# A grouped-query attention block with cached keys and values: how the last unit is divided and turned, and how the result is copied and stored

## The chip, the cores and the metric

The kernel runs on one core of one Trainium2 chip. The metric is the device time of one execution in microseconds; lower is better. A profiled execution gives a span (first to last instruction) and its own time, which is a little longer.

## The reference

Eight sequences, four new tokens each (32 token rows), 32 query heads that share 8 key/value heads, 2048 cached keys, head width 128. Everything is bf16.

```python
B, Sq, D = 8, 4, 512
Hq, Hkv, Sk, Dh = 32, 8, 2048, 128
q = (x @ wq).reshape(B, Sq, Hq, Dh).transpose(0, 2, 1, 3)
k = jnp.repeat(k_cache, 4, axis=1)
v = jnp.repeat(v_cache, 4, axis=1)
scores = jnp.einsum("bhqd,bhkd->bhqk", q, k) * (Dh ** -0.5)
p = softmax(scores, axis=-1)
o = jnp.einsum("bhqk,bhkd->bhqd", p, v)
return o.transpose(0, 2, 1, 3).reshape(B, Sq, Hq * Dh) @ wo
```

## The kernel before

The work is cut into 16 units. A unit is one sequence and four key/value heads: 64 query rows (four heads, each with 16 rows) against 2048 keys per head. Its keys and its values are 2 MB each and come in one transfer each; with `wq` and `wo` (4 MB each) the kernel reads 75.5 MB.

Per unit, the stages are: VectorE turns the keys in two halves (line 134), TensorE makes the scores, for one half of the keys on PSUM rows 0 to 63 and for the other half on rows 64 to 127 (L203), VectorE takes the maxima (L221 to L227), ScalarE the exponentials with their sums (L239), VectorE turns the probabilities (L249), and ScalarE, GpSimd and for the last unit VectorE spread them into a block form (L259). GpSimd adds the sums (L213, L272), VectorE inverts them (L277). Then 32 products accumulate the values into one PSUM tile `o_ps` (L288), 128 rows by two blocks of 128 columns. Of this tile two quarters are wanted: rows 0 to 63 of block 0 and rows 64 to 127 of block 1.

`divide` (L298 to L306) takes just these two quarters: two instructions of 64x128, each multiplied by the inverse sum of its row, into `o_sc` of 128x128. It is ScalarE's for units 0 to 13 and VectorE's for units 14 and 15. `finish` (L308 to L315) multiplies `o_sc` in fp32 by `both`, a 128x64 matrix that is the sum of the two halves of an identity (`ident4[:, :64] + ident4[:, 64:]`, L128). So the product turns `o_sc` and adds its two row halves in one go. The trace shows each fp32 product as two weight loads and two matmuls. A copy (L312) moves the result to `oT`; for units 13, 14 and 15 it is ScalarE's.

The order of instructions on each engine is the order of the program text, which the author wrote out by hand (`manual_schedule`). The unit loop runs 18 turns; in turn n the scores are of unit n and the values of unit n − 2. In the last turn the order is: values of unit 15, `finish(14)`, `divide(15)`. After the loop come, in this order: four row steps of the output projection (`project(0, 0, 4)`), `finish(15)`, four more row steps, then `to_tokens(1)` (eight transposes of `oT` into `nat`, two copies on ScalarE and VectorE, L330), four row steps, `to_wo_rows(1)` (eight products into `perm`, two copies, L348), and all the remaining row steps. A row step is two products of 32 output rows by 256 columns (L356), one for each half of the output columns, so the result `out_ps` stands as 64 rows by 256 columns. The weights `wo` arrive in six pieces issued by SyncE (L101); the last three hold 5, 2 and 1 row steps, and the last row step needs the last piece.

At the end two copies move `out_ps` to `out_sb`, one for each half of the columns: ScalarE, then VectorE (L419). Two stores follow: ScalarE's queue writes rows 0 to 31 into the left half of the output (L420), SyncE's queue rows 32 to 63 into the right half (L421).

Of the kernel before, what the change touches and what calls it, by code (L numbers as in the profile page):

```python
# [9 lines left out]
FP32 = mybir.dt.float32  # L10
# [4 lines left out]
def kernel(  # L15
# [9 lines left out]
    nc = tc.nc  # L25

    B, Sq, D = x.shape
    _, Hkv, Sk, Dh = k_cache.shape
# [3 lines left out]
    T = B * Sq  # L32
# [5 lines left out]
    NQ = G * HQ  # L38
# [4 lines left out]
    DH = D // 2  # L43
    NU = (Hkv // G) * B
# [14 lines left out]
    small = ctx.enter_context(tc.tile_pool(name="small", bufs=2))  # L59
# [13 lines left out]
    ident4 = const.tile([128, 128], FP32, name="ident4")  # L73
    both = const.tile([128, NQ], FP32, name="both")
# [3 lines left out]
    out_sb = const.tile([2 * T, DH], BF16, name="out_sb")  # L78
# [53 lines left out]
    def turn_keys(u, t):  # L132
        kts[(u, t)] = ktpool.tile([128, CT, 2, S, 2], BF16, tag="kt", name="kt")
        nc.vector.transpose(  # L134
            kts[(u, t)][:, :, :, :, :].rearrange("k c h s e -> k (c h s e)").bitcast(FP32),
            ks[u][:, t * CT : (t + 1) * CT, :].rearrange("s c d -> s (c d)").bitcast(FP32),
        )
# [11 lines left out]
    def q_products(hq):  # L149
        psq = psum_m.tile([128, rep * Dh], FP32, tag="m", name="psq")  # L150
        for r in range(R):
            for g in range(G):
                c0 = (hq * G + g) * rep * Dh
                nc.tensor.matmul(  # L154
                    psq[g * T : (g + 1) * T, :],
                    lhsT=xT_sb[:, r, :],
                    rhs=wq_sb[:, r, c0 : c0 + rep * Dh],
                    start=(r == 0),
                    stop=(r == R - 1),
                )  # L160
        return psq
# [10 lines left out]
    def spread_q(hq, q_nat, engines):  # L172
        q_t = small.tile([128, rep, 4, B, Sq], BF16, tag="q_t", name="q_t")
        nc.vector.transpose(  # L174
            q_t[:, :, :, :, :].rearrange("w h i b s -> w (h i b s)"),
            q_nat[:, :, :, :].rearrange("t n e w -> t (n e w)"),
        )
        for g in range(G):
            rows = slice(g * S, (g + 1) * S)
            engines[g](  # L180
                out=q_bd[rows, hq, :, :, :, g, :].rearrange(
                    "w k e b (h s) -> w (k e b) h s", h=rep
                ),
                in_=q_t[rows, :, :, :, :].rearrange("w h i b s -> w (i b) h s"),
            )
# [10 lines left out]
    def scores(u, t):  # L196
        hq, b = units[u]
        if t == 0:
            s_pss[u] = psum_s.tile([128, NT, CT // 2, S], FP32, tag="s", name="s_ps")
        for i in range(4):  # L200
            k, e = i // 2, i % 2
            for h in range(2):
                nc.tensor.matmul(  # L203
                    s_pss[u][h * NQ : (h + 1) * NQ, t, :, :],
                    lhsT=q_bd[:, hq, k, e, b, :, :].rearrange("k g q -> k (g q)"),
                    rhs=kts[(u, t)][:, h * CT // 2 : (h + 1) * CT // 2, k, :, e],
                    start=(i == 0),
                    stop=(i == 3),
                )
# [7 lines left out]
    def maxima(u):  # L217
        top = small.tile([128, 1], FP32, tag="top", name="top")
        swapped = small.tile([128, 1], FP32, tag="swapped", name="swapped")
        less[u] = small.tile([128, 1], FP32, tag="less", name="less")  # L220
        nc.vector.reduce_max(  # L221
            out=top[:, :],
            in_=s_pss[u][:, :, :, :].rearrange("q t c s -> q (t c s)"),
            axis=AX,
        )
        swap_halves(nc.vector, swapped, top)
        nc.vector.tensor_scalar(  # L227
            out=less[u][:, :],
            in0=swapped[:, :],
            scalar1=top[:, 0:1],  # L230
            scalar2=-1.0,
            op0=mybir.AluOpType.max,
            op1=MULT,
        )
# [12 lines left out]
    def probs_to_keys(u):  # L247
        p_t = small.tile([128, C // 4, 2, HQ, 2], BF16, tag="p_t", name="p_t")
        nc.vector.transpose(  # L249
            p_t[:, :, :, :, :].rearrange("s x g q j -> s (x g q j)").bitcast(FP32),  # L250
            s_sbs[u][:, :, :, :].rearrange("q a s j -> q (a s j)").bitcast(FP32),
        )
        by = [nc.scalar.copy, nc.gpsimd.tensor_copy] * G
        if u == NU - 1:
            by = [nc.vector.tensor_copy, nc.gpsimd.tensor_copy, nc.scalar.copy] * 3
        for h in range(2):
            for g in range(G):
                quad = 2 * h + g // 2
                by[h * G + g](  # L259
                    out=probs[u % PB][g * S : (g + 1) * S, h, :, :, g, :],  # L260
                    in_=p_t[quad * S : (quad + 1) * S, :, g % 2, :, :].rearrange(
                        "s x q j -> s x j q"
                    ),
                )

    r_sbs = {}

    def sums(u):
        swapped = small.tile([128, 1], FP32, tag="l_swapped", name="l_swapped")
        total = small.tile([128, 1], FP32, tag="l_total", name="l_total")  # L270
        swap_halves(nc.gpsimd, swapped, l_sbs[u])
        nc.gpsimd.tensor_tensor(out=total[:, :], in0=l_sbs[u][:, :], in1=swapped[:, :], op=ADD)  # L272
        return total

    def inverses(u, total):
        r_sbs[u] = totals.tile([128, 1], FP32, tag="r_sb", name="r_sb")
        nc.vector.reciprocal(r_sbs[u][:, :], total[:, :])  # L277

    o_pss = {}
    o_scs = {}  # L280

    def values(u, quarter):
# [3 lines left out]
        for a in range(CT // 4):  # L286
# [8 lines left out]
                stop=(c == C - 2),  # L295
            )

    def divide(u):  # L298
        o_scs[u] = small.tile([128, Dh], FP32, tag="o_sc", name="o_sc")
        for h in range(2):  # L300
            rows = slice(h * NQ, (h + 1) * NQ)
            to, of, by = o_scs[u][rows, :], o_pss[u][rows, h, :], r_sbs[u][rows, 0:1]
            if u < NU - LAG:
                nc.scalar.mul(out=to, in_=of, mul=by)  # L304
            else:
                nc.vector.tensor_scalar_mul(out=to, in0=of, scalar1=by)  # L306

    def finish(u):  # L308
        hq, b = units[u]
        o_t = psum_m.tile([128, NQ], FP32, tag="m", name="o_t")  # L310
        nc.tensor.matmul(o_t[:, :], lhsT=o_scs[u][:, :], rhs=both[:, :], start=True, stop=True)  # L311
        (nc.vector.tensor_copy if u < NU - LAG - 1 else nc.scalar.copy)(  # L312
            out=oT[hq][:, :, :, b, :].rearrange("d h p s -> d p h s"),
            in_=o_t[:, :].rearrange("d (p h s) -> d p h s", p=2, h=HP),
        )  # L315
# [49 lines left out]
    for n in range(NU + LAG):  # L365
        w = n - LAG
        if 0 < n <= NU:
            total = sums(n - 1)
        if 0 < n < NU:
            turn_keys(n, 0)  # L370
            turn_keys(n, 1)
        if n < NU:
            scores(n, 0)
        if w >= 1 and n < NU:
            finish(w - 1)
        if n < NU:
            scores(n, 1)
        if n == 2:
            q_ps = q_products(1)
        if n == 3:  # L380
            spread_q(1, q_nat, [by_gpsimd] * G)
        if 0 < n <= NU:
            probs_to_keys(n - 1)
            inverses(n - 1, total)
        if n < NU:
            maxima(n)
            exponentials(n)
        if n == 2:
            q_nat = scale_q(q_ps)
        if w == B + 1:  # L390
            to_tokens(0)
        if w == B + 2:
            to_wo_rows(0)
        if w >= 0:
            for quarter in range(4):
                values(w, quarter)
            if n >= NU:
                finish(w - 1)
            divide(w)
        load_ready(min(n + 1, NU), max(w + 1, 0))  # L400
        if n == NU - 1:
            assert not loads, loads
            for piece in pieces:
                load_wo(*piece)

    out_ps = psum_s.tile([2 * T, DH], FP32, tag="s", name="out_ps")
    half = WR // 2
    project(0, 0, half)
    finish(NU - 1)
    project(0, half, half)  # L410
    to_tokens(1)
# [2 lines left out]
    project(1, half, half)  # L414
    for piece in pieces[2:]:
        project(*piece)
    o2 = out.flatten_outer_dims()
    for c0, copy in ((0, nc.scalar.copy), (DH // 2, nc.vector.tensor_copy)):
        copy(out=out_sb[:, c0 : c0 + DH // 2], in_=out_ps[:, c0 : c0 + DH // 2])  # L419
    nc.scalar.dma_start(out=o2[:, :DH], in_=out_sb[:T, :])  # L420
    nc.sync.dma_start(out=o2[:, DH:], in_=out_sb[T:, :])  # L421


# [28 lines left out]
```

## Time and profile before

| | us |
|---|---|
| runs shown | 185.2, 190.14, 190.29 (median 190.14) |
| profiled execution, its own time | 185.48 |
| its span | 183.7 |
| keys turned, VectorE L134 | 72.0 busy |
| values, TensorE L288 | 62.9 busy |
| division, ScalarE L304 (64x128) | 0.363 each, 28 of them |
| division, VectorE L306 (64x128) | 0.350 each, 4 of them |
| last values end, first `out_ps` product starts | 174.2, 174.3 |
| last product of L356 ends | 180.6 |
| stores issued | 181.2 |

How lines of the profile are read here: a line of the timeline has the start in us from the span's start, the busy time of the merged instructions, the engine (PE is TensorE, PEld its weight loads, DVE is VectorE, ACT ScalarE, SP SyncE; a q behind the name is its DMA issue), the source line, the operation, the tile written and the tiles read, the shape, and how many. In brackets stands how long the engine was idle before and what ended that. "Issue" means that the profile shows nothing that was waited for. A line of transfers has the size and the us from issue to landing.

### The profile page before, as it was taken

The page shows a single profiled execution, that of the slowest core. Times are in us where ns is not written, and L with a number is a line of the kernel's source. Part 1 is how long each engine was busy: PE and PEld are TensorE (multiplying, and loading weights), DVE is VectorE, ACT ScalarE, POOL GpSimd, SP SyncE. Part 2 cuts the span into 40 slices and gives each one's busy share as a digit, 9 for nine tenths or more (in the row PEclk, how much of TensorE's full clock was granted, in tenths as well). Part 3 has the DMA queues.
Part 4 walks back from the last instruction along what each step waited for, and adds up shares of the span by engine and source line. Part 5 has one row for each costly group of instructions (what it writes and reads, how often), then busy time and mean ns, then how long its engine had stood idle before and what let it go on. Part 6 is the DMA issues. An engine that isn't in the chain of part 4 may idle for free.

```text
span 183.7 us, 2500 instructions
## 1 busy us (share of the span) xinstructions
PE 122.7 (67%) x932; PEld 79.9 (44%) x932; DVE 119.8 (65%) x157; ACT 77.5 (42%) x136; POOL 59.4 (32%) x127
## 2 busy tenths in 40 slices
PE   0000470739996887839597839596776988399993
PEld 0000130213774664626354615455463656268871
DVE  4180209796999989494958677676958594946220
ACT  2000203435565754907263634547281619074020
POOL 8900011425175451605151513232231506056000
PEclk9999998556999999996969997969997599969999
DMA  6999999999999999999999999999999999999990
GB/s 189 460 421 407 435 432 432 428 432 432 428 435 421 441 417 437 426 432 432 425 435 428 432 428 435 425 432 432 432 432 428 432 425 439 425 432 416 426 366 26
DMA packets 5770, 75.70 MB, mean 412 GB/s; under 512 B 672, under 2 KB 896, under 8 KB 1152
## 3 DMA queue, kind: packets, MB, share of 16 engines
q1 hardware_dynamic: 5712, 75.55, 96.8%
q8 instruction: 7, 0.11, 0.2%
q10 hardware_dynamic: 48, 0.02, 0.0%
q14 instruction: 3, 0.02, 0.0%
HBM read 75.53 MB, written 0.03 MB: 411 GB/s over the span
## 4 chain that ended last, share of the span: by engine, by line
DMA 56%; DVE 26%; PE 12%; issue 3%; POOL 1%; ACT 0%; SPq 0%
DMA k_sb<-in_k_cache_dram 39%; DVE kt L134 19%; DMA x_sb<-in_x_dram 9%; DMA v_sb<-in_v_cache_dram 8%; PE s_ps L203 5%; DVE top L221 3%; PE o_ps L288 2%; PE out_ps L356 2%; PE psq L154 1%; DVE swapped L213 1%; POOL q_bd L180 1%; DVE q_t L174 1%; DVE less L227 1%; DVE o_sc L306 0%; PE perm L341 0%
## 5 line engine op out<-in xcount | busy, mean ns | idle before, releaser
L134 DVE STREAM_TRANSPOSE kt<-k_sb 128x2048 f32<-128x2048 f32 x32 | 72.0, 2288 | 21.7 <-DMA k_sb<-in_k_cache_dram 21.7
L203 PE MATMUL s_ps<-kt,q_bd 128*64 128x512 bf16 x256 | 45.0, 483 | 38.5 <-DVE kt L134 35.5
L288 PE MATMUL o_ps<-v_sb,probs 128*128 128x256 bf16 x512 | 62.9, 285 | 0.2 <-DMA v_sb<-in_v_cache_dram 0.2
L259 ACT COPY probs<-p_t 32x512 bf16<-32x512 bf16 x62 | 38.1, 615 | 54.1 <-DVE r_sb L277 53.0
L288 PEld LDWEIGHTS <-probs 128*128 128x128 bf16 x512 | 51.1, 102 | 14.7 <-issue 6.9
L259 POOL COPY probs<-p_t 32x512 bf16<-32x512 bf16 x63 | 38.7, 614 | 58.3 <-DVE r_sb L277 55.9
L203 PEld LDWEIGHTS <-q_bd 128*64 128x64 bf16 x256 | 17.3, 126 | 56.0 <-issue 24.7
L221 DVE TENSOR_REDUCE top<-s_ps 128x1 f32<-128x1024 f32 x16 | 19.6, 1223 | 16.5 <-PE s_ps L203 16.5
L239 ACT ACTIVATE s_sb<-s_ps,less 128x1024 bf16<-128x1024 f32 x16 | 22.4, 1399 | 11.0 <-DVE less L227 10.8
L213 POOL COPY l_swapped<-l_sb 64x1 f32<-64x1 f32 x32 | 5.8, 182 | 32.4 <-ACT s_sb L239 31.7
L304 ACT ACTIVATE o_sc<-o_ps,r_sb 64x128 f32<-64x128 f32 x28 | 10.2, 363 | 7.4 <-PE o_ps L288 6.9
L144 PE MATMUL xtp<-ident,x_sb 32*128 32x32 bf16 x4 | 0.3, 194 | 18.6 <-DMA x_sb<-in_x_dram 18.6
L249 DVE STREAM_TRANSPOSE p_t<-s_sb 128x512 f32<-128x512 f32 x16 | 11.0, 689 | 1.6 <-ACT s_sb L239 1.6
L165 ACT ACTIVATE q_nat<-psq 128x512 bf16<-128x512 f32 x2 | 1.2, 590 | 19.1 <-PE psq L154 19.1
L180 POOL COPY q_bd<-q_t 32x512 bf16<-32x512 bf16 x6 | 3.8, 626 | 16.9 <-DVE q_t L174 16.7
L144 PEld LDWEIGHTS <-x_sb 32*128 32x128 bf16 x4 | 0.2, 113 | 18.5 <-DMA x_sb<-in_x_dram 18.5
L311 PEld LDWEIGHTS o_t<-both,o_sc 128*128 128x128 f32 x32 | 5.2, 204 | 6.8 <-issue 4.9
L311 PE MATMUL o_t<-both,o_sc 128*128 128x64 f32 x32 | 7.2, 310 | 0.2 <-DVE o_sc L306 0.2
L127 POOL MEMSET probs<- 128x4096 bf16 x2 | 7.0, 3512 | 0.0
L213 DVE COPY swapped<-top 64x1 f32<-64x1 f32 x32 | 4.7, 148 | 0.8
L306 DVE TENSOR_SCALAR o_sc<-o_ps,r_sb 64x128 f32<-64x128 f32 x4 | 1.4, 350 | 5.0 <-issue 3.4
L356 PE MATMUL out_ps<-wo_sb,oP 128*32 128x256 bf16 x64 | 4.5, 274 | 0.0
(33 smaller groups left out, 39.6 us busy)
## 6 DMA issues: line engine op xcount, KB each, us to landing
k_sb<-in_k_cache_dram SPq DMA_DIRECT2D x16, 2048.0 KB, 24.5
v_sb<-in_v_cache_dram SPq DMA_DIRECT2D x16, 2048.0 KB, 23.3
wq_sb<-in_wq_dram SPq DMA_DIRECT2D x1, 4096.0 KB, 17.2
wo_sb<-in_wo_dram SPq DMA_DIRECT2D x3, 1024.0 KB, 18.2
wo_sb<-in_wo_dram SPq DMA_DIRECT2D x1, 640.0 KB, 21.4
wo_sb<-in_wo_dram SPq DMA_DIRECT2D x1, 256.0 KB, 21.5
wo_sb<-in_wo_dram SPq DMA_DIRECT2D x1, 128.0 KB, 19.6
x_sb<-in_x_dram SPq DMA_DIRECT2D x1, 32.0 KB, 16.9
```

What stands on the lines that cost most here:

```text
L127: nc.gpsimd.memset(pr[:, :, :, :, :, :], 0.0)
L134: nc.vector.transpose(kts[(u, t)][:, :, :, :, :].rearrange("k c h s e -> k (c h s e)").bitcast(FP32), ks[u][:, t * CT : (t + 1) * CT, :].r ...
L203: nc.tensor.matmul(s_pss[u][h * NQ : (h + 1) * NQ, t, :, :], lhsT=q_bd[:, hq, k, e, b, :, :].rearrange("k g q -> k (g q)"), rhs=kts[(u, t) ...
L213: engine.tensor_copy(out=out[h * NQ : (h + 1) * NQ, :], in_=in_[(1 - h) * NQ : (2 - h) * NQ, :])
L221: nc.vector.reduce_max(out=top[:, :], in_=s_pss[u][:, :, :, :].rearrange("q t c s -> q (t c s)"), axis=AX,)
L239: nc.scalar.activation(out=s_sbs[u][:, :, :, :].rearrange("q a s j -> q a j s"), in_=s_pss[u][:, :, :, :].rearrange("q t (a j) s -> q (t a ...
L249: nc.vector.transpose(p_t[:, :, :, :, :].rearrange("s x g q j -> s (x g q j)").bitcast(FP32), s_sbs[u][:, :, :, :].rearrange("q a s j -> q ...
L259: by[h * G + g](out=probs[u % PB][g * S : (g + 1) * S, h, :, :, g, :], in_=p_t[quad * S : (quad + 1) * S, :, g % 2, :, :].rearrange("s x q ...
L288: nc.tensor.matmul(o_pss[u][:, :, :].rearrange("n j d -> n (j d)"), lhsT=probs[u % PB][:, h, t * CT // 4 + a, :, :, :].rearrange("s j g q ...
L304: nc.scalar.mul(out=to, in_=of, mul=by)
L311: nc.tensor.matmul(o_t[:, :], lhsT=o_scs[u][:, :], rhs=both[:, :], start=True, stop=True)
L356: nc.tensor.matmul(out_ps[half * T : (half + 1) * T, :], lhsT=oP[p // 2][:, r, p % 2, :], rhs=wo_sb[:, p * WR + r, half * DH : (half + 1) ...
```

## The change

For the last unit alone, the division is one ScalarE instruction over the whole PSUM tile, all 128 rows and both blocks, into a new fp32 tile `o_all` of 128x256. The unit's turn is then two accumulating fp32 products, one for each block, with one half of the identity each as the moving operand; the halves choose the wanted quarters. At the end, ScalarE alone copies the whole 64x256 result, and its queue issues one store for all 64 rows, whose destination is written with three dimensions: 2 column halves, 32 token rows, 256 columns.

```diff
+    def divide_all(u):
+        o_scs[u] = small.tile([128, 2, Dh], FP32, tag="o_all", name="o_all")
+        nc.scalar.mul(out=o_scs[u][:, :, :], in_=o_pss[u][:, :, :], mul=r_sbs[u][:, 0:1])
+
     def finish(u):
         hq, b = units[u]
         o_t = psum_m.tile([128, NQ], FP32, tag="m", name="o_t")
-        nc.tensor.matmul(o_t[:, :], lhsT=o_scs[u][:, :], rhs=both[:, :], start=True, stop=True)
+        if u == NU - 1:
+            for h in range(2):
+                nc.tensor.matmul(
+                    o_t[:, :],
+                    lhsT=o_scs[u][:, h, :],
+                    rhs=ident4[:, h * NQ : (h + 1) * NQ],
+                    start=(h == 0),
+                    stop=(h == 1),
+                )
+        else:
+            nc.tensor.matmul(o_t[:, :], lhsT=o_scs[u][:, :], rhs=both[:, :], start=True, stop=True)
...
-            divide(w)
+            (divide_all if w == NU - 1 else divide)(w)
...
-    o2 = out.flatten_outer_dims()
-    for c0, copy in ((0, nc.scalar.copy), (DH // 2, nc.vector.tensor_copy)):
-        copy(out=out_sb[:, c0 : c0 + DH // 2], in_=out_ps[:, c0 : c0 + DH // 2])
-    nc.scalar.dma_start(out=o2[:, :DH], in_=out_sb[:T, :])
-    nc.sync.dma_start(out=o2[:, DH:], in_=out_sb[T:, :])
+    nc.scalar.copy(out=out_sb[:, :], in_=out_ps[:, :])
+    nc.scalar.dma_start(
+        out=out.flatten_outer_dims().rearrange("t (h j) -> h t j", h=2), in_=out_sb[:, :]
+    )
```

## The prediction

> **What bounds the kernel now.** I read the page's shares first, then the last ten microseconds in order of time, then the transfers.
>
> ```profile
> span 183.7 us, 2500 instructions
> DMA  6999999999999999999999999999999999999990
> q1 hardware_dynamic: 5712, 75.55, 96.8%
> ```
>
> The DMA engines are busy in every slice but the last: the kernel streams caches and weights, and the compute follows. The change touches only the instructions after the last unit's values, so its worth is read from the last slices.
>
> ```profile
> 174.30 0.71 DVE L306 TENSOR_SCALAR o_sc<-o_ps,r_sb 64x128 f32<-64x128 f32 x2 [3.35 <-issue]
> 174.41 0.21 ACT L312 CAST oT<-o_t 128x64 bf16<-128x64 f32 x1 [3.79 <-PE o_t L311]
> 175.13 0.30 PEld L311 LDWEIGHTS o_t<-both,o_sc 128*128 128x128 f32 x2 [0.49 <-ACT oT L312]
> 175.16 0.41 PE L311 MATMUL o_t<-both,o_sc 128*128 128x64 f32 x2 [0.24 <-DVE o_sc L306]
> 175.49 0.61 PE L356 MATMUL out_ps<-wo_sb,oP 128*32 128x256 bf16 x8
> 175.60 0.21 ACT L312 CAST oT<-o_t 128x64 bf16<-128x64 f32 x1 [0.98 <-PE o_t L311]
> ...
> 176.03 0.47 PEld L325 LDWEIGHTS <-oT 128*64 128x64 bf16 x8 [0.21 <-ACT oT L312]
> ...
> 179.36 1.03 PEld L356 LDWEIGHTS <-oP 128*32 128x32 bf16 x15 [0.19 <-issue]
> 180.30 0.28 PE L356 MATMUL out_ps<-wo_sb,oP 128*32 128x256 bf16 x2
> 180.62 0.26 ACT L419 CAST out_sb<-out_ps 64x128 bf16<-64x128 f32 x1 [2.53 <-PE out_ps L356]
> 180.91 0.28 DVE L419 CAST out_sb<-out_ps 64x128 bf16<-64x128 f32 x1 [2.52 <-ACT out_sb L419]
> 181.22 0.35 SPq L421 DMA_DIRECT2D out_dram<-out_sb  x1
> 181.23 0.40 ACTq L420 DMA_DIRECT2D out_dram<-out_sb  x1
> ```
>
> Two things are to be seen. First, the two copies of the result run one after the other (180.62, 180.91), and both stores are issued only after the second. Second, the last pair of products starts at 180.30 although PE could have started it sooner. The transfer that it needs was issued, and landed, as the order of SyncE's issues and the list of transfers have it (the last column is us from issue to landing):
>
> ```profile
> 160.69 0.33 SPq L101 DMA_DIRECT2D wo_sb<-in_wo_dram  x1
> ```
>
> ```profile
> wo_sb<-in_wo_dram SPq DMA_DIRECT2D x1, 128.0 KB, 19.6
> ```
>
> It lands at 160.69 + 19.6 = 180.29. So PE's chain has slack in front of the last pair, and I work out how much. Eight products of L356 take 0.61 and one alone 0.274, so pairs follow at (0.61 − 0.274) / 3 = 0.11. PE stood still 0.19 before 179.36 (the weight load's idle time), so the eight pairs of the last weight pieces could have begun at 179.17, and the last of them at 179.17 + 7 × 0.11 = 179.94. **The slack is 180.30 − 179.94 = 0.36.** What the change adds to PE's chain shows only beyond that.
>
> **Part 1, the division of the last unit.** Removed: two VectorE instructions, 174.30 to 175.01. Added: one ScalarE instruction of 128x256. On ScalarE it stands behind the cast of unit 14 (174.41 to 174.62), so it starts at 174.64. Its time: 64x128 with a factor by partition takes 0.363 on ScalarE (L304); copies without one take 0.375 at 256 columns (oP) and 0.590 at 512 (q_nat), so 128 more columns cost 0.108, together 0.47. Bounds: 0.375 (the cast of the same shape) and 0.73 (two of 0.363). It ends at 175.11 and not at 175.01: +0.10 (bounds 0 to +0.36). The handoff: the load that follows VectorE's division starts 175.13 − 175.01 = 0.12 later, the one that follows ScalarE's cast 176.03 − 175.81 = 0.22: +0.10 (bounds 0 to +0.10). Behind the new instruction on ScalarE stands only the cast of unit 15, which needs its result anyway; VectorE's next work is at 176.71, so what leaves it gains nothing.
>
> **Part 2, the second product.** One product of this form holds PE from 175.13 to 175.49, 0.36, and there are two now; both need the whole division. +0.36 (bounds +0.30, its two weight loads, to +0.41, its two matmuls). Every later step (cast, nat, its copy, perm, its copy) moves with it; the 32-column products beside them were fillers and move too. Parts 1 and 2: 0.10 + 0.10 + 0.36 = 0.56 on PE's chain (bounds 0.30 to 0.87), less the slack: **+0.20** on the start of the last pair (bounds 0 to +0.51). Cover is the landing at 180.29; were it gone, all 0.56 would show.
>
> **Part 3, the copy.** Removed: 180.62 to 181.19, two copies and the wait between. Added: one ScalarE copy of 64x256. The cast of 128x256 (oP) takes 0.375, and the 64x128 copy 0.259; the width decides: 0.37, so the store is issued 0.57 − 0.37 = **0.20 earlier** (bounds −0.29, if it took the 0.28 of a 64x128 copy, to −0.05, if it cost two of 0.26). SyncE loses a store behind which only the end of the program stood: nothing.
>
> **Part 4, the store.**
>
> ```profile
> DMA packets 96, 0.03 MB, mean 13 GB/s; under 512 B 32, under 2 KB 96, under 8 KB 96
> q10 hardware_dynamic: 48, 0.02, 2.5%
> q1 hardware_dynamic: 48, 0.02, 2.5%
> out_dram<-out_sb SPq DMA_DIRECT2D x1, 16.0 KB, 1.4
> out_dram<-out_sb ACTq DMA_DIRECT2D x1, 16.0 KB, 1.6
> ```
>
> This is the stretch from 181.2 to 183.7. Each old store is 48 packets: 32 rows of 512 B and 16 small ones, so 16 shares of two rows. The page has 672 packets under 512 B for 42 transfers (32 of k and v, 6 of wo, wq, x, two stores), again 16 each. But every one of these transfers has an outermost count of 32 or 128. The new store's destination is written as 2 × 32 × 256: outermost 2. No row shows how such a transfer is shared out. If by the outermost count, two engines carry 32 rows each, one after another. Price of a row: 2 × 2.5% of 16 engines over 2.5 us is 2.0 us of engine time; for 96 packets alike 21 ns, or 31 ns if the 64 rows had it all. So 32 rows take 0.67 to 1.0 us, where the bytes now pass in 0.29 (the stretches show transfers from 182.06 to 182.35): +0.4 to +0.7, and **I take +0.6**. Ends: 0 if 64 rows are shared by 16 engines, as they now are in two stores; +2.0 if four rows in a line always take the present 0.29, so that 32 take 2.3. I take the shares by the outermost count because all 42 transfers shown are consistent with it and the new one differs in just that.
>
> By the row alone (16 shares each time) the sum would be 0.6 less. The Trainium skill, "DMA: Bandwidth & Descriptors", section "Why a DMA increments its semaphore by 16 and not by 1", says that the number of engines is the largest number up to 16 that divides the outermost counts of both sides, so two engines for 64 and 2; by it this change gives up 14 of 16 engines for its last transfer. The 16 small packets of each transfer agree with it, and no run shown has a count that would tell.
>
> **The sum.** +0.20 − 0.20 + 0.60 = +0.60. The profiled execution took 185.48 (span 183.7 and 1.78 around it), so **186.1 us**. The three runs shown are 185.2, 190.14 and 190.29: the profiled one lies 2.5% under their median and beside the lowest. Nothing in the profile tells where 5 us come from, and this change removes nothing of that size. Bounds in the likeliest case: 0 − 0.29 + 0.4 and 0.51 − 0.05 + 2.0, so 185.6 to 187.9.
>
> **Rivals.**
> - *The store is still shared by 16 engines.* For it: every transfer on the page shows 16 shares. Against: none has an outermost count of 2. Then +0.20 − 0.20 + 0 = 185.5, the change is a wash.
> - *Slower by over 2%: the rows of a share wait for each other.* If an engine had to see each 512 B row confirmed before the next, the place is the store and the price per row is the time from the last packet (182.35) to the landing (181.23 + 1.6 = 182.83), 0.48: 32 × 0.48 = 15 us, which gives about 200 us. It decides (2% of 185.5 is 3.7) from (3.7 + 0.29) / 32 = 0.125 us per row on, four times the row price above. Against it: 75.55 MB pass at 96.8% busy time, with no such wait between packets, and two rows per share now cost 0.29 in all.
> - *The time falls at the other level.* Two of three runs of the unchanged kernel took 190.1 to 190.3. With the same +0.6 that is 190.7 to 190.9. For it: it is what the runs show; against: the profiled execution and one run show 185.
>
> **How the numbers follow.** Likeliest case (two engines, level of the profile) 0.42; 16 engines at that level 0.14; the upper level 0.39, with either store; rows that wait for each other 0.03; something else 0.02. Leaving out no more than 2 in 10 needs both levels: 185.3 to 191.0. Within 2% (about what a measurement of this kernel can tell from no change) is nearly all of it when levels are alike, 0.72. Faster by over 2% comes only of a time at 185 to 186 set against the median of 190.14, which I give 0.17; slower is the reverse of that, 0.08, and the waiting rows, 0.03: 0.11. No step of the change makes it faster by 2%: its whole gain is bounded by 0.29.
>
> **What would show it.** Part 1: an o_all instruction on ScalarE of 0.47 from 174.6, and a weight load some 0.2 behind it. Part 2: two pairs of fp32 matmuls, then the first nat load near 176.6. Slack: the idle time before 179.36 is gone and the last pair starts near 180.5. Part 3: one copy of 0.37 with the store right behind. Part 4: two small packets in place of 32 and transfers for 0.7 to 1.0 us instead of 0.29; 16 small packets would speak for the first rival. The prediction is wrong if the landing of the last wo piece moves, or if any stage before 174 differs.

## The result and the profile after

| | before | changed |
|---|---|---|
| runs | 7 | 7 |
| median, us | 185.67 (185.2 to 190.29) | 186.55 (186.12 to 191.73) |
| ratio | 1 | 1.0043, 95% interval 1.0027 to 1.006 |

The kernel became 0.43% slower, 0.8 us. That is small, and it is clear of noise: the interval holds no 1. The ratio compares the executions near each kernel's lowest time, because some executions of either kernel take 3 to 6 us more, as the profiled one of the changed kernel did (191.02): in a stretch far ahead of the change its loads ran at 381 to 390 GB/s and not at about 430. Its tail is therefore read below by differences between neighbouring lines and not by its absolute times.

The first view is the timeline of the changed kernel from the last unit's division on, in the columns explained above:

```profile
179.03 0.21 ACT L326 CAST oT<-o_t 128x64 bf16<-128x64 f32 x1 [3.92 <-PE o_t L325]
179.27 0.47 ACT L300 ACTIVATE o_all<-o_ps,r_sb 128x256 f32<-128x256 f32 x1
179.79 0.52 PEld L317 LDWEIGHTS o_t<-ident,o_all 128*128 128x128 f32 x4 [0.54 <-ACT o_all L300]
...
180.49 0.21 ACT L326 CAST oT<-o_t 128x64 bf16<-128x64 f32 x1 [0.75 <-PE o_t L317]
180.92 0.47 PEld L339 LDWEIGHTS <-oT 128*64 128x64 bf16 x8 [0.21 <-ACT oT L326]
...
182.75 2.47 PE L370 MATMUL out_ps<-wo_sb,oP 128*32 128x256 bf16 x40
...
185.26 0.36 ACT L431 CAST out_sb<-out_ps 64x256 bf16<-64x256 f32 x1 [2.28 <-PE out_ps L370]
185.65 1.12 ACTq L432 DMA_DIRECT2D out_dram<-out_sb  x1
```

From the cast of unit 14 to the first load of the nat products it is 180.92 − 179.03 = 1.89; before it was 176.03 − 174.41 = 1.62. So the longer division and the second product cost PE's chain 0.27. The last 40 products show where that went:

```profile
177.86 2.72 PE L356 MATMUL out_ps<-wo_sb,oP 128*32 128x256 bf16 x40
```

That is the kernel before. The same 40 products took 2.72 there and take 2.47 here: 0.25 of waiting for the last pieces of `wo` has left them. The 0.27 were paid out of the wait.

The end is another matter. The issue of the store shows 1.12, where the two old ones showed 0.35 and 0.40. The transfers of the two kernels, each in 40 slices of 0.06 us counted from the issue of the (first) store, first before, then after:

```profile
GB/s 0 0 0 0 0 0 0 0 0 0 0 0 0 0 85 154 188 94 26 0 0 0 0 0 0 0 0 0 0 0 0 0 0 0 0 0 0 0 0 0
DMA packets 96, 0.03 MB, mean 14 GB/s; under 512 B 32, under 2 KB 96, under 8 KB 96
```

```profile
GB/s 0 0 0 0 0 0 0 0 0 0 0 0 0 0 0 0 0 0 0 0 0 17 26 9 17 51 34 51 34 51 43 43 43 43 43 43 0 0 0 0
DMA packets 66, 0.03 MB, mean 14 GB/s; under 512 B 2, under 2 KB 66, under 8 KB 66
```

Two things differ. The 64 rows now come with 2 small packets and not with 32, and pass mostly at 34 to 51 GB/s over 15 slices and not at up to 188 over 5: two engines carry them. And the first row moves in slice 22 and not in slice 15, some 0.44 later. In the trace of single packets the first row starts 0.85 after the issue before and 1.29 after it now; the rows take 0.29 and 0.89 from first to last, each row 0.027 on its engine. From the issue to the end of the span it was 2.48 and is 3.44: **the store costs 0.96 more.** The copy saves 0.21 of it (copy's start to the store's issue: 0.60 before, 0.39 now). That leaves 0.75, of the 0.8 measured.

### The profile page after: what moved, and what is told of

The parts are those of the page before. It is cut to its first block, busy times and chain, and to the rows that moved or that the text cites. A ratio compares the mean times of both kernels' runs of the same rounds, so it can differ in the third digit from the quotient of the medians.

```text
span 189.1 us, 2499 instructions
## 1 busy us (share of the span) xinstructions
PE 126.2 (67%) x934; PEld 81.1 (43%) x934; DVE 119.1 (63%) x154; ACT 78.0 (41%) x137; POOL 59.1 (31%) x127
## 4 chain that ended last, share of the span: by engine, by line
DMA 60%; DVE 20%; PE 15%; ACT 1%; POOL 1%; issue 1%; SPq 0%
DMA k_sb<-in_k_cache_dram 51%; DVE kt L134 17%; DMA x_sb<-in_x_dram 9%; PE o_ps L288 6%; PE s_ps L203 5%; DVE top L221 2%; PE out_ps L370 2%; PE psq L154 1%; POOL q_bd L180 1%; DVE swapped L213 0%; DVE q_t L174 0%; PE o_t L317 0%; PE perm L355 0%; DVE less L227 0%; ACT q_nat L165 0%
## 5 line engine op out<-in xcount | busy, mean ns | idle before, releaser
L203 PE MATMUL s_ps<-kt,q_bd 128*64 128x512 bf16 x256 | 46.4, 496 | 39.8 <-DVE kt L134 36.8
L288 PE MATMUL o_ps<-v_sb,probs 128*128 128x256 bf16 x512 | 63.9, 288 | 0.3 <-ACT oT L326 0.3
L221 DVE TENSOR_REDUCE top<-s_ps 128x1 f32<-128x1024 f32 x16 | 19.6, 1223 | 17.1 <-PE s_ps L203 17.1
## 6 DMA issues: line engine op xcount, KB each, us to landing
wo_sb<-in_wo_dram SPq DMA_DIRECT2D x1, 128.0 KB, 19.6
```

The source lines that it names most:

```text
L203: nc.tensor.matmul(s_pss[u][h * NQ : (h + 1) * NQ, t, :, :], lhsT=q_bd[:, hq, k, e, b, :, :].rearrange("k g q -> k (g q)"), rhs=kts[(u, t) ...
L221: nc.vector.reduce_max(out=top[:, :], in_=s_pss[u][:, :, :, :].rearrange("q t c s -> q (t c s)"), axis=AX,)
L288: nc.tensor.matmul(o_pss[u][:, :, :].rearrange("n j d -> n (j d)"), lhsT=probs[u % PB][:, h, t * CT // 4 + a, :, :, :].rearrange("s j g q ...
```

## Experiments

The first four take the change apart. Theory: the store is the whole loss, the chain is hidden. Rival: the chain on TensorE delays the end.

**Changed division, two stores.** The changed kernel with the old stores behind the one copy:

```diff
-    nc.scalar.dma_start(
-        out=out.flatten_outer_dims().rearrange("t (h j) -> h t j", h=2), in_=out_sb[:, :]
-    )
+    o2 = out.flatten_outer_dims()
+    nc.scalar.dma_start(out=o2[:, :DH], in_=out_sb[:T, :])
+    nc.sync.dma_start(out=o2[:, DH:], in_=out_sb[T:, :])
```

> The changed kernel with two stores of 32 rows again (left half by ScalarE's queue, right half by SyncE's), all else as changed. Store theory (the single store, from its issue to the end of the span, costs 3.45 where the two took 2.48, and the longer division and turn are hidden behind the last wo piece): the 0.97 are gone and the earlier copy is left, 0.2 faster than the kernel before, ratio 0.999. Chain theory (the one ScalarE division and the second product delay the end): 0.1 to 0.4 slower than before, ratio 1.0005 to 1.002.

Measured: 0.9988 (0.9971 to 1.0005), median of the six runs 185.35. The loss is gone with the one store. The interval just holds 1, so this version is not shown to beat the kernel before.

**Old division, one store.** The kernel before with only the changed copy and store.

> The kernel before with only the end changed: one ScalarE copy of 64x256 and the one store whose destination is 2 x 32 x 256. Store theory: as slow as the whole change, +0.76 (ratio 1.004); the issue takes about 1.1 us on ScalarE's queue, two small packets, transfers over 0.88 us. Chain theory: less than +0.5.

Measured: 1.0041 (1.0017 to 1.0065), as slow as the whole change. Its end:

```profile
180.50 0.37 ACT L417 CAST out_sb<-out_ps 64x256 bf16<-64x256 f32 x1 [2.52 <-PE out_ps L356]
180.89 1.13 ACTq L418 DMA_DIRECT2D out_dram<-out_sb  x1
```

The long issue is here too, with the old division; from it to the end of the span (184.34) it is 3.45.

**Changed division, old end.** The kernel before with only `divide_all` and the two products.

> The kernel before with only the last unit's division and turn changed (one ScalarE instruction, two products), the end as before. Store theory: the chain from the division to the nat products is 0.27 later than before, which is less than the 0.36 that PE has in front of the last pair; the pair still starts at the landing of the last wo piece, time as before (ratio 0.9995 to 1.0005). Chain theory: +0.27 to +0.56, ratio 1.0015 to 1.003.

Measured: 0.9996 (0.9972 to 1.002). The interval would not exclude the lower end of the rival, 0.27 us (1.0015), but the timeline is plainer:

```profile
178.92 0.21 ACT L326 CAST oT<-o_t 128x64 bf16<-128x64 f32 x1 [4.64 <-PE o_t L325]
...
180.82 0.47 PEld L339 LDWEIGHTS <-oT 128*64 128x64 bf16 x8 [0.21 <-ACT oT L326]
...
182.65 2.46 PE L370 MATMUL out_ps<-wo_sb,oP 128*32 128x256 bf16 x40
```

The chain is 1.90 long, 0.28 more than before, and the 40 products take 2.46, 0.26 less.

**Old division, one copy.** The kernel before with only the copy changed, two stores.

> The kernel before with only the copy changed: one ScalarE copy of 64x256, two stores as before. Both theories: 0.2 faster, ratio 0.999; the stores are issued 0.4 after the copy begins and not 0.6.

Measured: 1.0001 (0.9977 to 1.0025); the time cannot tell 0.2 us. The timeline does: the copy starts at 185.05 and the first store is issued at 185.44, 0.39 later, where it was 0.60. But from that issue to the end of the span it is 2.55 here, and 2.55 to 2.56 in the two other traces with one copy and two stores, against 2.48 and 2.49 in the two traces with two copies. So 0.07 of the 0.21 is lost again behind the issue, and no run shows why. Set against the stores behind one copy, the single store is 0.89 dearer and not 0.96; the 0.75 for copy and store together stays.

**The division done twice.** To see how much cover the chain has, the changed kernel with two stores and this edit:

```diff
-        nc.scalar.mul(out=o_scs[u][:, :, :], in_=o_pss[u][:, :, :], mul=r_sbs[u][:, 0:1])
+        for _ in range(2):
+            nc.scalar.mul(out=o_scs[u][:, :, :], in_=o_pss[u][:, :, :], mul=r_sbs[u][:, 0:1])
```

> The changed division and turn with the one copy and two stores, and the ScalarE division done twice, the second writing the same values over the first. Slack theory: the chain to the nat products is then 0.27 + 0.47 = 0.74 later than in the kernel before; 0.36 of it are hidden by the landing of the last wo piece, so the last pair starts about 0.4 after that landing, and the time is 0.4 above that of the one division with two stores (ratio to before about 1.001). Without slack: 0.47 above it; if the chain is not on the path at all: the same as with one division.

Measured: 1.0013 (0.999 to 1.0035). Its products and the landing of the last `wo` piece:

```profile
178.68 2.36 PE L371 MATMUL out_ps<-wo_sb,oP 128*32 128x256 bf16 x40
```

```profile
160.74 0.33 SPq L101 DMA_DIRECT2D wo_sb<-in_wo_dram  x1
```

```profile
wo_sb<-in_wo_dram SPq DMA_DIRECT2D x1, 128.0 KB, 19.6
```

The 40 products now run without a wait in 2.36; against 2.72 that is 0.36, just the slack that was worked out ahead. The piece lands at 160.74 + 19.6 = 180.34, and the last pair starts at 178.68 + 2.36 − 0.27 = 180.77, 0.43 later, as the slack theory had it. The ratio alone could not tell 0.4 us here: its interval holds 1, and it overlaps that of the version with one division. By the timeline the cover is real and ends at 0.36; the change uses 0.27 of it. It moves a little from one execution to the next: in the profile of the two-store version the values end 0.21 later than before, and there the products run without a wait too.

The other kernels measure the store by itself. All have the old division, and all but the first of them have one copy.

**Two halves side by side, one store of 32 rows.**

```diff
+    nc.scalar.copy(out=out_row[:, :DH], in_=out_ps[:T, :])
+    nc.scalar.copy(out=out_row[:, DH:], in_=out_ps[T:, :])
+    nc.scalar.dma_start(out=out.flatten_outer_dims(), in_=out_row[:, :])
```

> The division as before; two ScalarE copies of 32x256 bring both halves onto 32 rows of 512 columns, and one store writes 32 rows of 1024 B (outermost count 32 on both sides). Theory 1, shares by the outermost count: 16 small packets again, issue 0.39, transfers over about 0.3, from issue to the end of the span 2.4 to 2.5, so a single store costs nothing by itself; the second copy adds about 0.37, together 0.1 to 0.2 slower than before (ratio 1.001). Theory 2, one store in place of two is what costs: 3.4 from issue to the end, ratio 1.005.

Measured: 1.0018 (0.9989 to 1.0047); 16 small packets, 2.54 from issue to end. One store in place of two is not what costs. The second copy, 0.36, eats what the first saved.

**31 rows, four shares, eight shares.** These vary what a share holds. The edits are the destination, in turn `o2[:31, :256]`, then `"t (c j) -> c t j"` with c = 4 and 128 columns, then the same with c = 8 and 64 columns over 16 tokens; the last two store from a tile of 128 rows.

> The division as before; one copy, and one store of rows 0 to 30 of the left half alone (31 x 256; the rest of the output is not stored). If shares go by a common divisor of the outermost counts: one small packet, 31 rows of 512 B on one engine over some 0.85 us. If they go by rows: 16 small packets and 0.3. The issue: about 1.1 if it grows with the rows of one share (31 as against 32), about 0.4 if with the rows of the whole store (31 as against 64) or with its three dimensions (two here).

> The division as before; one copy, then one store of 128 rows of 128 columns from a tile whose lower half is zeros, its destination 4 x 32 x 128 (the output's columns are not in their places). Shares by the outermost count: 4 small packets, 32 rows of 256 B on each engine, transfers in 0.6 to 0.9. The issue: about 1.1 if it grows with the rows of one share (32 as before), about 2.6 if with all rows (128 against 64).

> As the one with four shares, but the destination is 8 x 16 x 64 over the first 16 tokens (the other tokens are not stored): 8 small packets, 16 rows of 128 B on each engine. The issue: 0.39 + 14/30 of 0.73 = 0.73 if it grows with the rows of one share (2 rows take 0.39, 32 take 1.12), 2.6 if with all 128 rows, 1.12 if the three dimensions are what costs.

| store | dimensions | small packets | issue | first row after issue | rows pass in | issue to end |
|---|---|---|---|---|---|---|
| two of 32 rows (before) | 2 | 16 each | 0.35, 0.40 | 0.85 | 0.29 | 2.48 |
| changed | 3 | 2 | 1.12 | 1.29 | 0.89 | 3.44 |
| 32 rows of 1024 B | 2 | 16 | 0.38 | 0.88 | 0.29 | 2.54 |
| 31 rows | 2 | 1 | 0.51 | 0.78 | 0.78 | 2.83 |
| 4 x 32 rows of 256 B | 3 | 4 | 1.14 | 1.30 | 0.53 | 3.10 |
| 8 x 16 rows of 128 B | 3 | 8 | 1.20 | 1.36 | 0.22 | 2.88 |
| 2 x 32 rows, by SyncE | 3 | 2 | 0.69 | 1.29 | 0.88 | 3.48 |
| 64 rows | 2 | 16 | 0.54 | 1.20 | 0.29 | 2.79 |
| 2 x 16 rows | 3 | 2 | 1.23 | 1.40 | 0.44 | 3.10 |
| 62 rows | 2 | 2 | 0.54 | 0.81 | 0.83 | 2.91 |
| 48 rows | 2 | 16 | 0.38 | 0.89 | 0.23 | 2.41 |

The number of shares came out each time as the largest number up to 16 that divides the outermost counts of both sides (31: 1; 128 and 4: 4; 128 and 8: 8). That is the rule of the Trainium skill, "DMA: Bandwidth & Descriptors", section "Why a DMA increments its semaphore by 16 and not by 1"; the traces here agree with it in all eleven stores. The issue did not grow with the rows of a share: 31 rows on one engine took 0.51, 16 rows on each of eight took 1.20. That theory fell.

**The same store by SyncE.** `nc.sync.dma_start` in place of `nc.scalar.dma_start`.

> The kernel before with one ScalarE copy and the same 2 x 32 x 256 store, issued by SyncE and not by ScalarE. If the long issue belongs to the shape of the store: 1.1 us on SyncE too, 3.4 from issue to the end. If it belongs to ScalarE's queue: about 0.35 and an end 0.4 sooner.

Neither was quite right. SyncE is busy for 0.69 and not for 1.12, but the first row still moves at 1.29 and the end comes after 3.48: the engine of the queue does not matter to the store's time, and the length of the issue is not what delays the rows.

**64 rows in two dimensions, 32 rows in three.** Until here the three-dimensional stores were also those with more than 32 rows. These two were to part that. The first writes `"t (h j) -> (t h) j"`, the second `o2[:16]` as 2 x 16 x 256.

> The kernel before with one ScalarE copy of 64x256 and one store of the 64 rows to 64 consecutive rows of 256 columns, two dimensions and not three (the rows' places in the output are not the reference's). So far stores of two dimensions and 31 or 32 rows had their first packet 0.78 to 0.88 after the issue, stores of three dimensions and 64 or 128 rows 1.29 to 1.36. If the dimensions cost: first packet at 0.85, 16 small packets, transfers over 0.3, 2.5 from issue to the end, time 0.2 below before. If the number of rows costs: first packet at 1.29 and 2.9 to the end.

> The kernel before with one ScalarE copy of 64x256 and one store of 32 rows as 2 x 16 x 256 over the first 16 tokens (the other half is not stored). Two small packets and 16 rows on each of two engines, transfers over 0.45. If the dimensions cost: first packet at 1.29 and 3.0 to the end. If the number of rows costs: first packet at 0.85 and 2.6 to the end.

Measured: 1.0007 (0.9992 to 1.0021) for the first. Both are late: 1.20 in two dimensions with 64 rows, 1.40 in three with 32. The second settles that more rows are not needed; the first left open whether rows delay it too. Its ratio, from six executions, does not show the gain of 0.2 us (0.9989) that an early first row would have given, which speaks against an accident of the one execution that was traced.

**62 and 48 rows in two dimensions.** The first rows of the 64-row store, `[:62]` and `[:48]`.

> The kernel before with one ScalarE copy and one store of 62 rows to 62 consecutive rows of 256 columns, two dimensions (two rows are not stored and the others are not in the reference's places). 62 has only 2 as a divisor up to 16: two small packets, 31 rows on each of two engines, transfers over 0.85. What it tells is the time from the issue to the first packet: 1.29 and an issue of 1.1 if two shares of some 30 rows cause both; 1.2 and 0.54, as for 64 rows in two dimensions, if the third dimension is what makes the issue long and the rows delay the first packet.

> As that one with 48 rows (16 shares of three). If the time to the first packet grows with the rows of the store (0.88 for 32, 1.20 for 64): 1.04. If it jumps with the rows of a share or with the number of rows above 32: 1.2; if only 64 is late: 0.85.

The 62-row store is close to the changed one without its third dimension: two engines, 31 rows each. Both views are in slices of 0.06 us from the issue; first 62 rows, then 2 x 16 rows in three dimensions:

```profile
187.20 0.54 ACTq L418 DMA_DIRECT2D out_dram<-out_sb  x1
```

```profile
GB/s 0 0 0 0 0 0 0 0 0 0 0 0 0 26 26 17 26 43 51 43 43 43 43 43 43 43 43 0 0 0 0 0 0 0 0 0 0 0 0 0
DMA packets 64, 0.03 MB, mean 13 GB/s; under 512 B 2, under 2 KB 64, under 8 KB 64
```

```profile
186.69 1.23 ACTq L418 DMA_DIRECT2D out_dram<-out_sb  x1
```

```profile
GB/s 0 0 0 0 0 0 0 0 0 0 0 0 0 0 0 0 0 0 0 0 0 0 0 34 26 34 43 43 43 43 9 0 0 0 0 0 0 0 0 0
DMA packets 34, 0.02 MB, mean 7 GB/s; under 512 B 2, under 2 KB 34, under 8 KB 34
```

With almost twice the rows, the two-dimensional store moves its first row in slice 14, one before the old ones, and the three-dimensional one in slice 24. Neither forecast for the 62 rows was right: the issue took 0.54, but the first row came at 0.81. So two shares alone do not delay the first row, and with 32 rows, few enough to be early in two dimensions (0.85 and 0.88), the third dimension is enough to delay it (1.40).

Measured against the 62-row store, the changed store's 0.96 come apart: 3.44 − 2.91 = 0.53 with the third dimension, 2.91 − 2.48 = 0.43 with the two shares. What stays open is the 1.20 of the 64-row store: 48 and 62 rows in the same form took 0.89 and 0.81, so it does not grow with rows. The changed store has 64 rows too. That its late first row comes of the third dimension alone, and not in part of what delays the 64 rows in two dimensions, is therefore not shown. How far single traces can be trusted: the two traces of the changed store have the first row at 1.29 both times, the five of the two plain stores at 0.85 each time.

## Why the prediction was right or wrong

The total, +0.6 us, was near the +0.8 measured, and 186.1 near 186.55; the sign of the sum was right. That it came so near was partly luck: what the chain adds to the end was put 0.20 too high and the store 0.36 too low, and the two errors cancel in part. Wrong too was the reading of the sum. The prediction filed +0.3% under no change, because it took 2% as what a measurement of this kernel can tell. The measurement tells more than that: its interval is 0.33% wide, and 0.43% is a slowdown.

- Part 1: the one ScalarE division was forecast at 0.47 and took 0.473; it ended 0.11 later than VectorE's two (+0.10 forecast). The handoff was forecast +0.10 slower than VectorE's; it is 179.79 − 179.74 = 0.05, so faster than the 0.12 before and outside the bounds of 0 to +0.10. The row it was taken from was a load of bf16 weights behind a cast, the load here is of fp32 weights; no run shows whether that is the reason.
- Part 2: the second product was forecast at +0.36, the whole of one. Two take 0.59 (179.79 to 180.38 in the timeline, where the next products start), +0.23, below the bounds of +0.30 to +0.41. Behind the first product the second added 0.22 to the loads (0.30 to 0.52) and 0.25 to the matmuls (0.41 to 0.66), side by side; the price of a product that stands alone was too high for it. So the chain grew by 0.11 − 0.07 + 0.23 = 0.27 and not by 0.56.
- The slack in front of the last pair was forecast at 0.36, and the doubled division measured 0.36. With the smaller chain the whole of parts 1 and 2 is hidden, about 0 in place of +0.20 on the end.
- Part 3: −0.20 forecast, −0.21 measured.
- Part 4 is the step that failed. The shares were right (2 small packets, two engines) and so was the price of the rows: +0.6 forecast, 0.89 − 0.29 = 0.60 measured. But the step priced only the rows. It put the change in the time from the issue to the first row at nothing, without a reason, and that time grew from 0.85 to 1.29: +0.96 in place of +0.6. The experiments show that a third dimension is enough for such a delay; whether the 64 rows had a part in it here stays open. The bounds of the step (0 to +2.0) held it, for another reason than they gave.
- The rivals: 16 engines fell (2 small packets). Rows that wait for each other fell (0.027 each, one behind the other). The upper level was not where the median fell.

## What to carry to other kernels

Look at a store's destination as the instruction carries it: an outermost count of 2 put 64 rows on two engines, and the first row of the three-dimensional store came 0.44 us later, so that one store was 0.96 us dearer than two plain ones that ran side by side on two queues. At the end of this kernel nothing hid that, while 0.27 us of added work on TensorE's chain was free, because the last weight piece landed later still. When a change is worth less than a percent, price it against the spread of comparable runs and not against a general threshold.

## What was not expected of the hardware

A store with a destination of three dimensions moved its first row 1.29 to 1.40 us after its issue in all six stores that had one, whatever its rows (32 to 128), shares (2 to 8) and queue; in two dimensions it was 0.78 to 0.89 in five of six forms and 1.20 in the sixth (64 rows), which stays unexplained. The busy time of the issue on ScalarE was 1.12 to 1.23 in the five three-dimensional stores that ScalarE issued, while SyncE shows 0.69 for the same store and the same first row at 1.29.
